# A third buffer for the output rows, a later place for the copies of v, and another cut of the last rows

## The chip, the cores and the metric

The kernel runs on one core of a Trainium2 chip. The metric is the device time of one execution in microseconds (us). A core has five engines that run their own instruction queues in order and meet at semaphores: TensorE (PE in the profile; its weight loads are shown apart as PEld), VectorE (DVE), ScalarE (ACT), GpSimd (POOL) and SyncE (SP, which here issues DMAs only).

## The reference, cut to what is computed

Sliding-window causal attention over 8 batches of 8 heads, 576 positions, head size 64, window 64, and then a layer x → (h·cos h)·w_out with h = x·w_in over the 4608 rows of 512 that come out of it.

```python
scores = scale * np.matmul(q, k.transpose(0, 1, 3, 2))
mask = (rel >= 0) & (rel < window)          # rel = row position - column position
scores = np.where(mask, scores, -1000000000.0)
attn = np.exp(scores - max); attn = attn / (sum + 1e-09)
x = np.matmul(attn, v)                      # 8 batches -> (4608, 512), heads side by side
h = x @ w_in                                # 512 -> 2048
out = (h * np.cos(h)) @ w_out               # 2048 -> 512, float32
```

## The kernel before

**Stages.** The 4608 rows are worked in nine stages of 512 rows (`mt`, 0 to 8). A stage has a first half, in which `h_ps` = w_in × xT is made for 16 blocks of 128 features (four matmuls of 512 columns each, L425), ScalarE takes the sine (L553; the cosine as a sine with an offset) and VectorE multiplies (L556, `gT`), and a second half, in which four blocks of 128 output rows are made, 16 matmuls of 512 columns each (L567). Each block is copied out of PSUM into half of a tile `out_sb` of 128 × 2 × 512 (L571): the even blocks by VectorE, the odd ones by ScalarE. Two blocks share one tile; in all stages but the last the tile is stored by one DMA of 512 KB that SP issues (`store`, L443), which is planned half a step to one step into the next stage. The pool has two buffers for these tiles (tag "out"). At the very start the same two buffers hold the plain float32 rows of q and k of the first two heads (`load_plain`, L160).

**Attention.** It runs a stage ahead: in stage t the attention of batch t + 1 is made while the matmuls above run. A batch has 8 heads in 4 pairs and 9 blocks of 64 rows; a unit is one pair and one block, a group three or four units, ten groups a batch. For a group TensorE makes the scores (L284), VectorE adds the mask and takes the maximum (L304), ScalarE takes exponentials and sums (L315), VectorE the reciprocals (L322), GpSimd multiplies (`g_norm`, L329, "normalisation", tile `w`), and SP issues a DMA transpose of `w` into `wT` (L341). At the end of a stage TensorE multiplies `wT` with v for the next stage's 512 rows (`values`, L356, 4 pairs of 16 matmuls), and the results are copied to `xT` (`put_x`, L361).

**q, k, v.** GpSimd issues the DMA loads, which cast to bfloat16: q and k in chunks of 96 rows two stages ahead of use (L174; 12 a stage), v in five chunks one stage ahead (L180). k is transposed by DMA on SP (`turn_k`, L244, six a batch), q on TensorE. A block of rows needs v of its own and of the preceding 64 positions, so a tile of v has 8 slots of 128 rows that overlap by 64: DMA fills the even slots, and `spread_v` (L184) builds the odd ones from them with two copies, one for each half of the partitions (64 × 1536 and 64 × 2048 elements). For batches 3 to 7 GpSimd makes these copies, one pair in each of stages 2 to 6.

**What sets the order.** Each engine runs its instructions in the order of the program. For the first stage that order is written out by hand (`FIRST`, L47). After it a list of steps with times (`at`, L449) is drained in order of time by `pump` (L452) between the matmuls of a stage; a stage is T = 32 units of planned time and t0 is its start. In stage t the groups' scores are planned from t0 + 14.6 on, 0.36 units for each unit of attention, the maxima 0.2, the exponentials 1, the reciprocals 3, the normalisations 3.2 and the transposes 3.8 later. The loads of q and k lie at t0 + 5.6 to 14.4, and the two copies of v at t0 + 14.45 and 14.55 (L492), ahead of the first normalisation.

**Which groups a stage's end needs.** In stages 3 to 6 the values of the next stage need the first four groups of the new batch; the other six belong to rows of the stage after. In stage 2 they need the first six (`CUTS`, L29).

**The last rows.** The last 128 rows of the last stage are split by columns (`last_rows`, L432): 16 matmuls for the first 448 columns, then 16 for the last 64. ScalarE copies and stores the first part, VectorE copies and SP stores the second.

Of the kernel before, what the change touches and what calls it, by code (L numbers as in the profile page):

```python
# [14 lines left out]
F32 = mybir.dt.float32  # L15
BF16 = mybir.dt.bfloat16
# [7 lines left out]
NU = 9  # L24
NC, NP = 6, 96
GF = 4
LAST = 448
PACE = 0.36
CUTS = (  # L29
# [7 lines left out]
RC = 9  # L37
PAIRS = 4
# [2 lines left out]
LAGS = (0.2, 1, 3, 3.2, 3.8)  # L41
SKEW = 3
DIRECT = (0, 7, 8)

# [28 lines left out]
def kernel(  # L73
# [10 lines left out]
    B, H, S, D = q.shape  # L84
    assert (B, H, S, D) == (8, 8, 576, 64)
    scale = 1.0 / math.sqrt(D)
    d_model = H * D
# [7 lines left out]
    const = ctx.enter_context(tc.tile_pool(name="const", bufs=1))  # L95
    ld = ctx.enter_context(tc.tile_pool(name="ld", bufs=2))
    att = ctx.enter_context(tc.tile_pool(name="att", bufs=3))
    moe = ctx.enter_context(tc.tile_pool(name="moe", bufs=2))
    ps = ctx.enter_context(tc.tile_pool(name="ps", bufs=1, space=PSUM))
    ps_t = ctx.enter_context(tc.tile_pool(name="ps_t", bufs=3, space=PSUM))  # L100

    qtiles = [const.tile([128, S], BF16, name=f"qT{i}") for i in range(2 * PAIRS)]
    qblocks = [const.tile([128, NU, 2, 64], BF16, name=f"qB{i}") for i in range(2 * PAIRS)]
    vtiles = [const.tile([128, NU - 1, d_model], BF16, name=f"v{i}") for i in range(2)]
    w_in_sb = const.tile([128, PAIRS, d_ff], BF16, name="w_in")
# [9 lines left out]
    st = {}  # L115
# [9 lines left out]
    def bank(which, name):  # L125
        return ps.tile([128, 512], F32, tag=which, name=name)

    def copy(engine, out, in_):
        {"a": nc.scalar.copy, "p": nc.gpsimd.tensor_copy}.get(engine, nc.vector.tensor_copy)(out, in_)  # L129
# [28 lines left out]
                            in_=src.rearrange("(a h) (p c) d -> (h p) a (c d)", h=2, c=RC))  # L158

    def load_plain(name):  # L160
        rows = moe.tile([128, 2, d_model], F32, tag="out", name="rows", bufs=2).rearrange("p a f -> p (a f)")[:, 0:RC * D]
        st["rows", name] = rows
        nc.sync.dma_start(out=rows, in_={"q": q, "k": k}[name][0, 0:2].rearrange("h (p c) d -> (h p) (c d)", c=RC))

# [94 lines left out]
    for b, cuts in enumerate(CUTS, 2):  # L259
        for cut in cuts:  # L260
            for p0 in range(0, PAIRS, 2):
                for of, lo, hi in cut:
                    groups += [[(b, p, j) for p in range(p, p + of) for j in range(lo, hi)] for p in range(p0, p0 + 2, of)]
    direct = set(range(n_first)) | {n_first + i for i in DIRECT}

# [144 lines left out]

    def put_out(m, engine=None):
        if ("osb", m // 2) not in st:
            st["osb", m // 2] = moe.tile([128, 2, d_model], F32, tag="out", name="out_sb", bufs=2)
        copy(engine, st["osb", m // 2][:, m % 2], st.pop(("out", m)))

    def exp_table():
        nc.scalar.activation(small, small, AF.Exp, scale=0.0)
# [4 lines left out]
    def first(mt, ff, ks, start, stop):  # L422
        if start:
            st["h", ff] = bank(H_BANKS[mt == 1][ff], "h_ps")
        nc.tensor.matmul(out=st["h", ff], lhsT=w_in_sb[:, ks, ff * 128:ff * 128 + 128],  # L425
                         rhs=st["xT", mt][:, ks], start=start, stop=stop)

    def skewed(mt, ks, n):
        for ff in range(SKEW):
            first(mt, ff, ks, n == 0, n == PAIRS - 1)  # L430

    def last_rows(gT, o_sb):  # L432
        ms = MT // 128 - 1
        for which, lo, hi in (("O0", 0, LAST), ("S", LAST, d_model)):
            o_ps = bank(which, "out_ps")[:, lo:hi]
            for ff in range(n_ff):
                nc.tensor.matmul(out=o_ps, lhsT=gT[ff // 2][:, ff % 2, ms * 128:ms * 128 + 128],  # L437
                                 rhs=w_out_sb[:, ff, lo:hi], start=ff == 0, stop=ff == n_ff - 1)
            to = moe.tile([128, MT], F32, tag="sin", name="last_sb", bufs=4)[:, lo:hi] if lo else o_sb[:, 1, lo:hi]
            copy("d" if lo else "a", to, o_ps)  # L440
            (nc.sync if lo else nc.scalar).dma_start(out=out[n_mt * MT - 128:n_mt * MT, lo:hi], in_=to)

    def store(o_sb, mt, ms0, e, n):  # L443
        r0 = mt * MT + (ms0 + e) * 128
        nc.sync.dma_start(out=out[r0:r0 + n * 128].rearrange("(a p) f -> p a f", p=128), in_=o_sb[:, e:e + n])
# [3 lines left out]
    def at(time, fn, *args):  # L449
        plan.append((time, len(plan), fn, args))  # L450

    def pump(time):  # L452
        plan.sort(key=lambda x: x[:2])
        while plan and plan[0][0] <= time:
            _, _, fn, args = plan.pop(0)
            fn(*args)
# [20 lines left out]
    for b in range(2, B):  # L477
        t0 = T * (b - 1)
        for p in range(PAIRS):
            t_q = t0 + (2 if b == 2 else 1) + (3.3 if b == 2 else 3.5) * p  # L480
            for lag, fn, *args in ((0, tr_q), (0.02, put_block, 0), (0.5, put_block, 1)):
                at(t_q + lag, fn, b, p, *args)
        if b > 2:
            for c in range(NC):
                for i, name in enumerate(("q", "k")):
                    at(t0 - T + 5.6 + 1.6 * c + 0.8 * i, load_chunk, name, b, c)
        for c in range(NC):
            at(t0 + (2 + 1.2 * c if b == 2 else c - 5.5), turn_k, b, c)
        for c in range(5):
            at(t0 + 0.5 + c, load_v, b, c)  # L490
        for half_ in range(2):
            at(t0 + (14.45 + 0.1 * half_ if b > 2 else 10), spread_v, b, half_, "p" if b > 2 else "s")  # L492
    for mt in range(2, n_mt):
        for p in range(PAIRS):
            time = T * mt - (8.01 if mt == n_mt - 1 else 1.01)
# [11 lines left out]
    def spread_first(lo, hi):  # L507
        return lambda i, engine: spread_v(0, i, engine, lo, hi)

    steps = {"Lq0": lambda p: load_heads("q", 0, p, 1) if p else load_plain("q"),  # L510
             "Lk0": lambda p: load_heads("k", 0, p, 1) if p else load_plain("k"),
             "cq": lambda engine: cast_plain("q", engine), "ck": lambda engine: cast_plain("k", engine),
             "Lq1": lambda p: load_heads("q", 1, p, 1), "Lk1": lambda p: load_heads("k", 1, p, 1),
# [23 lines left out]
    for mt in range(1, n_mt):  # L537
        base = mt * T
        gT = []
        for ks in range(PAIRS):  # L540
            pump(max([base - 1] + [time for time, _, fn, args in plan if fn is put_x and args[:2] == (mt, ks)]))
            skewed(mt, ks, ks)
        for ff in range(n_ff):
            for ks in range(PAIRS):
                if ff >= SKEW:
                    first(mt, ff, ks, ks == 0, ks == PAIRS - 1)
            h_ps = st.pop(("h", ff))
            sin = moe.tile([128, MT], F32, tag="sin", name="sin", bufs=4)
            if ff % 2 == 0:
                gt = moe.tile([128, 2, MT], BF16, tag="gT", name="gT", bufs=n_ff // 2 + 2)  # L550
                gT.append(gt)
            e = ff % 2
            nc.scalar.activation(sin, h_ps, AF.Sin, bias=math.pi / 2.0)  # L553
            if ff == n_ff - 1 and mt < B - 1:
                exp_table()
            nc.vector.tensor_tensor(out=gt[:, e], in0=h_ps, in1=sin, op=ALU.mult)  # L556
            pump(base + ff)
        for ms0 in range(0, MT // 128, 2):
            o_sb = moe.tile([128, 2, d_model], F32, tag="out", name="out_sb", bufs=2)
            o_ps = [bank(which, "out_ps") for which in (("O1",) if mt == n_mt - 1 and ms0 else ("O1", "O0"))]  # L560
            for e in range(2):
                ms = ms0 + e
                if mt == n_mt - 1 and ms == MT // 128 - 1:
                    last_rows(gT, o_sb)
                    break
                for ff in range(n_ff):
                    nc.tensor.matmul(out=o_ps[e], lhsT=gT[ff // 2][:, ff % 2, ms * 128:ms * 128 + 128],  # L567
                                     rhs=w_out_sb[:, ff], start=ff == 0, stop=ff == n_ff - 1)
                    if ff % 4 == 3:
                        if ff == n_ff - 1:  # L570
                            copy("a" if e else "d", o_sb[:, e], o_ps[e])  # L571
                            if mt == n_mt - 1:
                                store(o_sb, mt, ms0, e, 1)
                        pump(base + Q + 4 * ms0 + (e * n_ff + ff) // 4)
            if mt < n_mt - 1:
                at(base + T + 0.5 + ms0 / 2, store, o_sb, mt, ms0, 0, 2)
# [30 lines left out]
```

## Time and profile before

| | |
|---|---|
| time, three runs | 312.56, 314.43, 317.30 us; median 314.43 |
| profiled execution | 314.01 us, of which the span from first to last instruction 312.2 |
| busy time | TensorE 299.8, ScalarE 236.2, VectorE 229.4, GpSimd 192.3 us |
| DMA queues | GpSimd's 18.06 MB (84.4% of 16 engines' span), SP's 22.36 MB (36.9%) |
| L567 and L425, 1008 matmuls of 512 columns | 117.3 and 116.0 us busy |
| L329 normalisations on GpSimd | 75, mean 963 ns |
| L129 copies of v on GpSimd | 10, mean 1684 ns |
| L341 and L244, DMA transposes on SP | 68 of w and 36 of k, 3.9 and 7.5 us from issue to landing (median) |
| L445 stores of 512 KB on SP | 16, 7.8 us from issue to landing (median) |

The stages' bounds in the trace are 57.92 (stage 1), 90.50, 122.70, 154.74, 187.84, 220.04, 252.04 (stage 7) and 281.07 us (stage 8). A line of a timeline has start, duration, engine, source line, operation, output and inputs, and in brackets how long the engine sat idle before it and what ended that. L129 is the copy helper, so the tile tells which copy it is. An x2 means that two instructions are merged in one line. A line of the chain has start, duration and what ran. A line of the waits has the waiting instruction, what it waited for, the total, how often, and the longest.

### The profile page before, as it was taken

The page shows a single profiled execution, that of the slowest core. Times are in us where ns is not written, and L with a number is a line of the kernel's source. Part 1 is how long each engine was busy: PE and PEld are TensorE (multiplying, and loading weights), DVE is VectorE, ACT ScalarE, POOL GpSimd, SP SyncE. Part 2 cuts the span into 40 slices and gives each one's busy share as a digit, 9 for nine tenths or more (in the row PEclk, how much of TensorE's full clock was granted, in tenths as well). Part 3 has the DMA queues.
Part 4 walks back from the last instruction along what each step waited for, and adds up shares of the span by engine and source line. Part 5 has one row for each costly group of instructions (what it writes and reads, how often), then busy time and mean ns, then how long its engine had stood idle before and what let it go on. Part 6 is the DMA issues. An engine that isn't in the chain of part 4 may idle for free.

```text
span 312.2 us, 7988 instructions
## 1 busy us (share of the span) xinstructions
PE 299.8 (96%) x2659; PEld 161.5 (52%) x2659; DVE 229.4 (73%) x877; ACT 236.2 (76%) x785; POOL 192.3 (62%) x227
## 2 busy tenths in 40 slices
PE   3889999999999999999999899999999999999995
PEld 3668844545554555555555455454545554454443
DVE  5998988599769966897679667977698768235701
ACT  4998799777996799779977798689969986116600
POOL 8988666984679696958795978886842630000000
PEclk9979999999999999999999999999999999999999
DMA  8999999999979994999599979999894342011011
GB/s 158 178 217 170 200 177 140 122 143 194 219 108 142 159 191 78 133 128 231 88 116 129 228 109 100 135 228 123 99 127 151 68 117 91 0 69 68 0 69 67
DMA packets 155162, 41.17 MB, mean 132 GB/s; under 512 B 143408, under 2 KB 150384, under 8 KB 155120
## 3 DMA queue, kind: packets, MB, share of 16 engines
q0 software_dynamic: 100192, 18.06, 84.4%
q1 hardware_dynamic: 54784, 22.36, 36.9%
q8 instruction: 21, 0.34, 0.5%
q14 instruction: 21, 0.17, 0.2%
q10 hardware_dynamic: 144, 0.23, 0.2%
HBM read 36.70 MB, written 9.44 MB: 148 GB/s over the span
## 4 chain that ended last, share of the span: by engine, by line
PE 87%; DMA 4%; POOL 4%; DVE 1%; ACT 1%; issue 1%; DVEq 0%; POOLq 0%; ACTq 0%
PE h_ps L425 34%; PE out_ps L567 32%; PE h_ps L389 5%; PE s_ps L284 4%; PE out_ps L408 4%; PE o_ps L356 3%; DMA out_dram<-out_sb 3%; PE tq_ps L211 2%; POOL w L329 2%; DMA q<-in_q_dram 2%; POOL v L180 1%; PE out_ps L437 1%; PE s_ps L290 1%; PE tw_ps L338 1%; PE o_ps L375 1%
## 5 line engine op out<-in xcount | busy, mean ns | idle before, releaser
L567 PE MATMUL out_ps<-w_out,gT 128*128 128x512 bf16 x496 | 117.3, 379 | 0.0
L425 PE MATMUL h_ps<-xT,w_in 128*128 128x512 bf16 x512 | 116.0, 379 | 0.2
L315 ACT ACTIVATE e<-s,negm 128x128 f32<-128x128 f32 x256 | 98.7, 387 | 3.9 <-DVE negm L304 3.9
L553 ACT ACTIVATE sin<-h_ps 128x512 f32<-128x512 f32 x128 | 73.8, 598 | 32.1 <-PE h_ps L425 29.7
L556 DVE TENSOR_TENSOR gT<-h_ps,sin 128x512 bf16<-128x512 f32 x128 | 81.6, 685 | 21.8 <-ACT sin L553 21.0
L329 POOL TENSOR_TENSOR w<-e,rden 128x512 bf16<-128x512 f32 (+1 forms) x75 | 71.4, 963 | 32.9 <-DVE rden L322 26.3
L425 PEld LDWEIGHTS <-w_in 128*128 128x128 bf16 x512 | 48.5, 98 | 53.8 <-issue 0.4
L567 PEld LDWEIGHTS <-gT 128*128 128x128 bf16 x496 | 45.9, 98 | 44.2
L304 DVE CUSTOM_DVE_ANT_0 s<-s_ps,mask 128x128 f32<-128x128 f32 x256 | 58.2, 285 | 1.2 <-PE s_ps L290 1.0
L315 ACT ACTIVATION_READ_ACCUMULATOR e<-s,negm 128x1 f32 x256 | 47.8, 187 | 0.0
L174 POOL DMA_DIRECT2D q<-in_q_dram x36 | 28.5, 792 | 11.1 <-DMA q<-in_q_dram 5.3
L180 POOL DMA_DIRECT2D v<-in_v_dram x40 | 34.0, 866 | 0.6 <-DMA v<-in_v_dram 0.3
L174 POOL DMA_DIRECT2D k<-in_k_dram x36 | 28.3, 787 | 8.3 <-DMA k<-in_k_dram 4.4
L129 ACT COPY out_sb<-out_ps 128x512 f32<-128x512 f32 (+1 forms) x18 | 10.2, 567 | 25.0 <-PE out_ps L567 18.4
L322 DVE RECIPROCAL rden<-den 128x4 f32<-128x4 f32 (+1 forms) x79 | 13.6, 172 | 19.4 <-ACT e L315 18.9
L129 DVE COPY out_sb<-out_ps 128x512 f32<-128x512 f32 x18 | 12.4, 690 | 19.7 <-PE out_ps L567 12.0
L284 PEld LDWEIGHTS <-qB 128*128 128x128 bf16 x216 | 16.9, 98 | 15.8 <-DVE negm L304 2.4
L284 PE MATMUL s_ps<-kT,qB 128*128 128x128 bf16 x216 | 21.9, 219 | 1.0 <-DVE negm L304 0.9
L129 DVE COPY qB<-tq_ps 64x576 bf16<-64x576 bf16 x48 | 21.6, 450 | 0.3
L304 DVE DVE_READ_ACCUMULATOR2_ANT negm<- 128x1 f32 x256 | 21.3, 83 | 0.0
L129 DVE CAST xT<-o_ps 128x512 bf16<-128x512 f32 x24 | 15.5, 678 | 6.7 <-PE o_ps L356 6.7
L129 POOL COPY v<-v 64x1536 bf16<-64x1536 bf16 (+1 forms) x10 | 16.8, 1684 | 4.9 <-DMA v<-in_v_dram 4.6
(64 smaller groups left out, 253.4 us busy)
## 6 DMA issues: line engine op xcount, KB each, us to landing
out_dram<-out_sb SPq DMA_DIRECT2D x16, 512.0 KB, 7.8
v<-in_v_dram POOLq DMA_DIRECT2D x32, 128.0 KB, 5.7
q<-in_q_dram POOLq DMA_DIRECT2D x36, 96.0 KB, 9.1
k<-in_k_dram POOLq DMA_DIRECT2D x36, 96.0 KB, 8.9
w_in<-in_moe_w_in_dram POOLq DMA_DIRECT2D x4, 512.0 KB, 8.5
w_out<-in_moe_w_out_dram POOLq DMA_DIRECT2D x4, 512.0 KB, 10.8
wT<-w SPq DMA_TRANSPOSE x68, 3.9
q<-in_q_dram POOLq DMA_DIRECT2D x7, 144.0 KB, 5.6
```

The source lines that it names most:

```text
L129: {"a": nc.scalar.copy, "p": nc.gpsimd.tensor_copy}.get(engine, nc.vector.tensor_copy)(out, in_)
L174: nc.gpsimd.dma_start(out=st[name, b][:, c].rearrange("p (h d) -> p h d", h=H), in_=src.rearrange("h p d -> p h d"))
L180: nc.gpsimd.dma_start(out=vt.rearrange("p (h d) -> p h d", h=H), in_=v[b, :, c * 128:c * 128 + n, :].rearrange("h p d -> p h d"))
L284: nc.tensor.matmul(out=s_ps[:, u].rearrange("p (a t) -> p a t", a=2), lhsT=qblocks[(b % 2) * PAIRS + p][:, j].rearrange("d h t -> d (h t)" ...
L304: nc.vector.tensor_tensor_reduce(out=s[:, u], in0=s_ps[:, u], in1=mask[:, 2 - j % 2 if j else 0], scale=-scale if b else -1.0, scalar=BIG, ...
L315: nc.scalar.activation(e[:, u], s[:, u], AF.Exp, bias=negm[:, u:u + 1], scale=1.0 if n < n_first else -1.0, accum_out=den[:, u:u + 1])
L329: (nc.gpsimd if engine == "p" else nc.vector).tensor_tensor(out=w[:, 0:u], in0=e[:, 0:u], op=ALU.mult, in1=rden[:, 0:u].unsqueeze(2).to_br ...
L389: nc.tensor.matmul(out=h_ps[:, half * e:half * e + half], lhsT=w_in_sb[:, ks, ff * 128:ff * 128 + 128], rhs=st["xT", 0][:, ks, half * g:ha ...
L425: nc.tensor.matmul(out=st["h", ff], lhsT=w_in_sb[:, ks, ff * 128:ff * 128 + 128], rhs=st["xT", mt][:, ks], start=start, stop=stop)
L553: nc.scalar.activation(sin, h_ps, AF.Sin, bias=math.pi / 2.0)
L556: nc.vector.tensor_tensor(out=gt[:, e], in0=h_ps, in1=sin, op=ALU.mult)
L567: nc.tensor.matmul(out=o_ps[e], lhsT=gT[ff // 2][:, ff % 2, ms * 128:ms * 128 + 128], rhs=w_out_sb[:, ff], start=ff == 0, stop=ff == n_ff - 1)
```

## The change

Three edits, cut from the diff:

```diff
-LAST = 448
+LAST = 384
...
+OUTS = 3
...
-    qtiles = [const.tile([128, S], BF16, name=f"qT{i}") for i in range(2 * PAIRS)]
+    first_q = moe.tile([128, 2, d_model], F32, tag="out", name="qT", bufs=OUTS).rearrange("p a f -> p (a f)").bitcast(BF16)
+    qtiles = [first_q[:, S * i:S * i + S] for i in range(PAIRS - 1)]
+    qtiles += [const.tile([128, S], BF16, name=f"qT{i}") for i in range(PAIRS - 1, 2 * PAIRS)]
...
-        rows = moe.tile([128, 2, d_model], F32, tag="out", name="rows", bufs=2).rearrange("p a f -> p (a f)")[:, 0:RC * D]
+        rows = moe.tile([128, 2, d_model], F32, tag="out", name="rows", bufs=OUTS).rearrange("p a f -> p (a f)")[:, 0:RC * D]
...
-            st["osb", m // 2] = moe.tile([128, 2, d_model], F32, tag="out", name="out_sb", bufs=2)
+            st["osb", m // 2] = moe.tile([128, 2, d_model], F32, tag="out", name="out_sb", bufs=OUTS)
...
-            at(t0 + (14.45 + 0.1 * half_ if b > 2 else 10), spread_v, b, half_, "p" if b > 2 else "s")
+            at(t0 + (22.2 + 0.1 * half_ if b > 2 else 10), spread_v, b, half_, "p" if b > 2 else "s")
...
-            o_sb = moe.tile([128, 2, d_model], F32, tag="out", name="out_sb", bufs=2)
+            o_sb = moe.tile([128, 2, d_model], F32, tag="out", name="out_sb", bufs=OUTS)
```

The tag "out" gets three buffers in place of two. Each is 4096 bytes a partition; to make room, the transposed q of the first three pairs of batch 0 (3 × 1152 bytes), which had tiles of their own for the whole kernel, lies in the first of the three buffers until the first output rows take it over. The pair of copies of v of batches 3 to 7 is planned at t0 + 22.2 and 22.3, between the fourth normalisation (t0 + 22.12, in stage 2 t0 + 21.4) and the fifth. The last 128 rows are split into 384 and 128 columns.

## The prediction

> **What bounds the kernel now.** I read the table of engines first (TensorE busy for 299.8 of the 312.2 us span), then the stretches of stages 2 to 6, the steady ones in which the change works (stage = the loop variable mt; the cuts are where the chain shows the first h_ps group of each).
>
> ```profile
> core 0: us, PE busy (x) PEld busy (x) DVE busy (x) ACT busy (x) POOL busy (x), PEclk, DMA share, GB/s
> 90.50:122.70 32.20, 32.18 (x254) 16.76 (x254) 25.50 (x112) 28.08 (x97) 26.01 (x30) 1.00 1.49 140
> 122.70:154.74 32.04, 32.01 (x253) 16.52 (x254) 25.28 (x112) 26.72 (x92) 26.12 (x29) 1.00 1.54 142
> 154.74:187.84 33.10, 32.14 (x252) 16.57 (x252) 25.50 (x112) 27.38 (x95) 26.23 (x29) 1.00 1.54 142
> 187.84:220.04 32.20, 32.14 (x252) 16.56 (x253) 25.51 (x112) 27.39 (x95) 26.02 (x29) 1.00 1.63 144
> 220.04:252.04 32.00, 31.97 (x252) 16.66 (x253) 25.83 (x112) 27.99 (x98) 17.31 (x18) 1.00 0.81 111
> ```
>
> The reader is to see that a stage lasts as long as its matmuls, about 32.0 us at a granted clock of 1.00, except stage 4, which lasts 33.10. No other engine reaches 29 us. So there is little to win: what lies above 32.0 is 0.20, 0.04, 1.10, 0.20 and 0. The chain of waits says what the 1.10 is, and the list of waits how often its cause occurs:
>
> ```profile
> 167.16 1.74 PE h_ps L425 x8
> 169.09 7.99 DMA out_dram<-out_sb
> 177.33 0.45 issue
> 178.82 0.40 PE s_ps L284 x4
> ```
> ```profile
> DVE out_sb L129 <- DMA out_dram<-out_sb: 7.2, 4, 2.6
> PE s_ps L284 <- DVE negm L304: 0.9, 1, 0.9
> ```
>
> The stores of the stage before stand in SP's queue behind ten transposes of w and six of k, and in stage 4 are issued at 169.09, 14 us into the stage. They land 8 to 9 us later, and the first output copy of the stage, on VectorE, needs that buffer. The timelines of VectorE and TensorE there, and GpSimd's:
>
> ```profile
> 177.17 0.69 DVE L129 COPY out_sb<-out_ps 128x512 f32<-128x512 f32 x1 [2.56 <-DMA out_dram<-out_sb]
> 178.82 0.40 PE L284 MATMUL s_ps<-kT,qB 128*128 128x128 bf16 x4 [0.94 <-DVE negm L304]
> ```
> ```profile
> 173.54 3.43 POOL L129 COPY v<-v 64x1536 bf16<-64x1536 bf16 x2
> 177.06 3.03 POOL L329 TENSOR_TENSOR w<-e,rden 128x512 bf16<-128x512 f32 x3
> ```
>
> VectorE stands still for 2.56 us; behind the copy in its queue lie the reciprocal and the maxima of the next groups, so a bank of scores is freed late and TensorE stops. The same wait lasts 1.43, 1.55 and 1.65 us in stages 2, 3 and 5 and hardly reaches TensorE (in stage 5 one group of four score matmuls takes 0.40 us of the chain in place of 0.22). So some 1.5 us of such a wait is covered, and all beyond it costs TensorE one for one: 2.56 - 1.5 = 1.06.
>
> **Part 1, the third buffer.** Buffers now go round in three: the first pair of rows of a stage takes the buffer of the second pair of two stages earlier, whose store landed a stage ago; the second pair takes that of the first pair of the stage before. The closest case is stage 4: that store is issued at 169.09, lands by 178.1, and the copy that needs it is the third of the stage, which came after 180.94. So all four waits (7.2 us of VectorE) go. Worth on TensorE: 1.0 us in stage 4 (33.10 less the mean 32.15 of stages 2, 3 and 5 is 0.95; by the cover 1.06) and 0.2 in stage 5 (0.40 - 0.22): 1.2. The ends are 0.95 (stage 4 alone) and 1.54 (each of the four falls to stage 6's 32.00). What is late next is nothing on VectorE; TensorE's own matmuls are.
>
> The price is that three tiles of q of batch 0 share the first buffer. The first output copy, at 46.09, must then wait for their last score matmuls; those (group 8, eight matmuls) ended at 43.83 and stand ahead of the matmuls that the copy waits for anyway: 0. The plain rows of q and k take buffers 2 and 3 at the start, both free: 0. Whether a write of one of the three q tiles waits for reads of another the trace can't show. Upper end: the second VectorE write (9.66 to 10.40) would wait for the scores that end at 10.35, 0.7 us, on a start whose chain runs through loads and GpSimd; lower end 0, since nothing gets earlier. I take 0: kT and xT are written by slices of one tile in the same way, and no wait of a writer for a reader of another slice is listed.
>
> **Part 2, the two copies of v.** Nothing is added: ten instructions stay ten, and no DMA moves. In stages 2 to 6 the pair (3.43 us in stage 4, 3.41 in stage 6) moves past four normalisations on GpSimd; no load lies between. The first normalisation of stage 4 then needs only its reciprocal (173.54) and starts at about 173.8, not 177.06. With ScalarE's pace of 1.54 us a group (four exponentials at 0.387) the fourth ends at 179.6, the copies at 183.1, and the fifth starts at 183.2, not 181.2. SP hardly feels it: its transposes take 1.2 to 2.4 us each, and in the old order it fell behind GpSimd with every one (the fifth normalisation of stage 4 was done at 182.2, its transpose issued at 184.48). The new order has the first four early and the fifth at 184.3. The tenth normalisation waits for its reciprocal (188.55) in both orders, so the loads behind it don't move. What waits for the copies are the value matmuls at the stage's end. Ends of the copies, from each stage's own reciprocals, against first use (a stage's TensorE moved earlier by its saving): 117.6 against 121.3, 150.7 against 153.6, 183.1 against 185.6, 216.1 against 218.7, 248.2 against 250.9. The least margin is 2.5 us. Cover is thinner in stage 2: there the values also need groups 5 and 6, and the sixth transpose, issued at 119.68, is what the value matmuls wait for now (a piece of 0.02 us of issue at 122.12 in the chain). The sixth normalisation would end at 119.4 and not at 117.06, and SP take it at 119.5 to 119.8: between -0.2 and +0.3 us, I take 0.1. Sum of part 2: +0.1, ends -0.2 and +0.5.
>
> One sentence from the Trainium skill speaks against moving GpSimd's work about: SBUF — State Buffer, section "Who interferes with whom", says that VectorE and GpSimd share a port pair, and that a VectorE instruction with two SBUF inputs, or in a two-port mode, shuts GpSimd out for its whole length. By that rule with such neighbours the pair could take twice 3.43 us; here the rule and the rows agree on no loss, since the maxima (s_ps and mask) and the output copies (out_ps) that lie beside the new place read at most one operand from SBUF.
>
> **Part 3, the last rows.** The chain gives 3.51 us for the 32 matmuls. At the 512-column rate (0.86 us for four) 16 of 448 columns are 3.02, which leaves 0.49 for those of 64. New: 16 of 384 are 2.59 and, at the rate of the 128-column scores (0.22 for four), 16 of 128 are 0.88: 3.47, so -0.04. VectorE's last copy took 0.225 us for 64 columns and 0.690 for 512, so 128 take 0.29: +0.07. ScalarE's part ends 0.45 earlier, but the other store is last (issued 309.02 against 308.87). Landing: 2.1 us for 32 KB, 2.0 for 256 KB, so 64 KB cost nothing. Sum +0.03, ends -0.2 and +0.2 (the landing's spread on both sides).
>
> DMA: Bandwidth & Descriptors of the Trainium skill, section "Specifications", puts the line rate at runs of 512 B and more; the last store goes from 256 to 512 B a row, which by that rule would be a gain. The two landings of 2.1 and 2.0 us leave no more than 0.1 for it.
>
> **Sum.** The profiled execution took 314.01 us: span 312.2 and 1.81 around it. 314.01 - 1.2 + 0.1 + 0.03 = 312.9; I forecast 312.8, since the three runs shown (312.56, 314.43, 317.30) spread over 4.7 us and every microsecond by which a store lands later than here would have cost one in up to four stages, and that source goes. The median of the runs, 314.43, is 0.4 above the profiled execution.
>
> **Rivals.**
> - The gain is given back. Groups 5 and 6 behind the copies hold the end of stage 2 (up to 0.5), the shared q buffer holds the start (up to 0.7): 312.9 + (0.5 - 0.1) + 0.7 = 314.0, no change. For it: stage 2 has no slack at its end now. Against: SP was 2.6 us behind GpSimd there.
> - The copies of v become the wait (the other side). If the pair takes 6.9 us and not 3.43, the values of stages 3 to 6 start 0.5, 0.9, 0.8 and 0.7 us late and stage 2's sixth group 3.4: 6.3, so 319.1, slower. It decides once the pair ends 2.5 us later than I have it, through length or a late start. Against: the pair lasted 3.43 beside maxima and 3.41 beside gating products; a late start of GpSimd by up to 2 us falls into the gaps of 0.5 us between its normalisations.
> - The third buffer changes nothing, because the wait is for something else. Against: the lines name the store, and 169.09 + 8 is 177.1. Then 314.1.
> - More than forecast: in the runs shown late stores cost more than in the profiled one, and the ends of the sums fall well: 314.01 - 1.54 - 0.2 - 0.2 = 312.1; from the fastest run, 312.56 less 1.2 is 311.4.
>
> **How the numbers follow.** Forecast (312.2 to 313.5): 0.55. Given back (313.5 to 315): 0.15; nothing done: 0.05. More than forecast (311.3 to 312.2): 0.13. Copies of v late (315 and up): 0.10; something unseen: 0.02. Range 311.3 to 315.0, which holds 0.88 before I allow for the runs' own spread; it is nearer 0.8 with it. The forecast's own range is 312.2 to 313.5. Two per cent, 6.3 us, is about what a measurement of this kernel can tell from no change; faster by that needs more than all that stages 2 to 6 have above 32.0 each (only the unseen: 0.02), and slower needs the copies later still than in the rival (half of its chance: 0.05), so within 2% has 0.93.
>
> **What would show it.** Part 1 is right if no output copy waits for a store and stage 4 lasts 32.1 us; wrong if VectorE still waits there, or SP's order has shifted the stores. Part 2 is right if four normalisations precede each pair, the pair still takes 3.4 us, and the value matmuls of stages 2 to 6 show no new wait; the sixth transpose of stage 2 should start at 119.5 to 119.8 less any shift. Part 3 is right if 32 matmuls take about 3.47 us and the last store ends the run. The prediction is wrong above all if the end of a stage waits for v or for wT.

## The result and the profile after

The changed kernel takes 312.72 us (median of 22 runs, 311.29 to 314.00), the kernel before 314.49 us (22 runs, 312.56 to 319.90). The ratio is 0.9933 with a 95% interval of 0.9913 to 0.9952, a gain of 0.5 to 0.9%, so within the 2% bound. Ratios and their intervals are estimated from the fast runs alone (runs over 1.5% above the fastest of their kernel count as slow), so they are not the quotients of the medians. The profiled execution after took 313.61 us with a span of 311.8, against 314.01 and 312.2 before.

The stretches of stages 2 to 6 of after, with the columns as before (length first, then busy time and instructions of each engine):

```profile
core 0: us, PE busy (x) PEld busy (x) DVE busy (x) ACT busy (x) POOL busy (x), PEclk, DMA share, GB/s
92.11:124.11 32.00, 31.76 (x249) 16.63 (x253) 25.71 (x112) 27.97 (x98) 26.05 (x30) 1.00 1.46 142
124.11:156.10 31.99, 31.75 (x249) 16.64 (x252) 25.74 (x112) 27.36 (x95) 25.76 (x29) 1.00 1.64 144
156.10:188.09 31.99, 31.76 (x248) 16.65 (x252) 25.74 (x112) 27.37 (x95) 26.13 (x30) 1.00 1.59 144
188.09:220.09 32.00, 31.76 (x249) 16.66 (x253) 25.83 (x112) 27.37 (x95) 26.12 (x30) 1.00 1.49 146
220.09:252.08 31.99, 31.75 (x249) 16.63 (x252) 25.88 (x112) 27.36 (x95) 16.89 (x18) 1.00 0.82 109
```

All five stages last 32.0 us; the 33.10 of stage 4 is gone. The third buffer is seen at work in VectorE's timeline of stage 4, and the new place of the copies in GpSimd's:

```profile
175.89 0.68 DVE L132 COPY out_sb<-out_ps 128x512 f32<-128x512 f32 x1
```
```profile
175.16 1.04 POOL L332 TENSOR_TENSOR w<-e,rden 128x512 bf16<-128x512 f32 x1
176.74 1.04 POOL L332 TENSOR_TENSOR w<-e,rden 128x512 bf16<-128x512 f32 x1 [0.54 <-DVE rden L325]
178.24 1.04 POOL L332 TENSOR_TENSOR w<-e,rden 128x512 bf16<-128x512 f32 x1 [0.46 <-DVE rden L325]
179.78 1.04 POOL L332 TENSOR_TENSOR w<-e,rden 128x512 bf16<-128x512 f32 x1 [0.50 <-DVE rden L325]
180.76 3.41 POOL L132 COPY v<-v 64x1536 bf16<-64x1536 bf16 x2
184.25 4.18 POOL L332 TENSOR_TENSOR w<-e,rden 128x384 bf16<-128x384 f32 x5
```

The output copy has no bracket, so VectorE didn't idle before it, though the two stores of the stage before were issued at 169.94 and 170.58 and took 8.4 and 9.4 us to land, as late as ever and after that copy had begun. Four normalisations precede the pair of copies, the second to the fourth waiting only for their reciprocals, and five run in one piece behind it.

But the span is only 0.4 us shorter, because this execution began worse. Its chain at the end of the first stage:

```profile
52.22 5.68 DMA wT<-w
57.95 0.66 PE o_ps L359 x30
```

TensorE waited 1.46 us for a transposed tile of w. Stage 1 began at 59.86, and at 58.19 in the execution before. The experiments show how much that varies.

The tail. First the DMA issues of before (last column: us from issue to landing), then the timeline and the DMA issues of after:

```profile
out_dram<-out_sb ACTq DMA_DIRECT2D x1, 224.0 KB, 2.1
out_dram<-last_sb SPq DMA_DIRECT2D x1, 32.0 KB, 2.1
```

```profile
308.42 0.37 ACTq L444 DMA_DIRECT2D out_dram<-out_sb  x1
309.13 0.33 SPq L444 DMA_DIRECT2D out_dram<-last_sb  x1
```
```profile
out_dram<-out_sb ACTq DMA_DIRECT2D x1, 192.0 KB, 1.9
out_dram<-last_sb SPq DMA_DIRECT2D x1, 64.0 KB, 1.6
```

Before, both stores landed in 2.1 us and were issued 0.15 us apart (308.87 and 309.02); now they are 0.71 apart and take 1.9 and 1.6. From the start of the last 32 matmuls, as the chain gives it, to the end of the span it is 311.8 - 305.28 = 6.52 us, against 312.2 - 305.24 = 6.96.

### The profile page after: what moved, and what is told of

It is laid out like the page before. It is cut to its first block, busy times and chain, and to the rows that moved or that the text cites. A ratio compares the mean times of both kernels' runs of the same rounds, so it can differ in the third digit from the quotient of the medians.

```text
span 311.8 us, 7954 instructions
## 1 busy us (share of the span) xinstructions
PE 296.8 (95%) x2627; PEld 161.6 (52%) x2659; DVE 230.6 (74%) x877; ACT 236.1 (76%) x785; POOL 191.7 (61%) x227
## 4 chain that ended last, share of the span: by engine, by line
PE 83%; DMA 8%; ACT 3%; POOL 3%; DVE 1%; issue 1%; SPq 1%; POOLq 0%; DVEq 0%; ACTq 0%
PE h_ps L428 34%; PE out_ps L570 34%; DMA w_in<-in_moe_w_in_dram 4%; PE s_ps L287 4%; PE h_ps L392 3%; PE o_ps L359 3%; ACT e L318 2%; PE tq_ps L214 2%; DMA wT<-w 2%; DMA k<-in_k_dram 2%; POOL v L183 1%; PE out_ps L440 1%; PE out_ps L411 1%; DVE s L307 1%; SPq L344 1%
## 5 line engine op out<-in xcount | busy, mean ns | idle before, releaser
L570 PE MATMUL out_ps<-w_out,gT 128*128 128x512 bf16 x482 | 116.1, 379 | 0.8 <-issue 0.2
L559 DVE TENSOR_TENSOR gT<-h_ps,sin 128x512 bf16<-128x512 f32 x128 | 81.6, 685 | 21.4 <-ACT sin L556 20.6
L307 DVE CUSTOM_DVE_ANT_0 s<-s_ps,mask 128x128 f32<-128x128 f32 x256 | 58.5, 286 | 1.2 <-PE s_ps L293 1.0
```

The lines of the kernel that those rows point to most:

```text
L307: nc.vector.tensor_tensor_reduce(out=s[:, u], in0=s_ps[:, u], in1=mask[:, 2 - j % 2 if j else 0], scale=-scale if b else -1.0, scalar=BIG, ...
```

## The experiments

All stages are measured alike in what follows: from the start of a stage's first h_ps matmul in TensorE's timeline to the next one's. "Tail" is the end of the span less the start of the last 32 matmuls in the chain; the span is printed to 0.1 us, so a tail is good to about 0.05. For each kernel one profiled execution is measured; medians are of its timed runs, with the ratio to runs of the kernel before that were timed beside them (the experiments' had medians of 313.98 to 314.35).

| kernel | stage 1 begins | stages 1, 2, 3, 4, 5, 6 (us) | tail | median or one run | ratio (95%) |
|---|---|---|---|---|---|
| before | 58.19 | 32.26, 32.17, 32.12, 33.10, 32.20, 32.00 | 6.96 | 314.49 | |
| after | 59.86 | 32.25, 32.00, 31.99, 31.99, 32.00, 31.99 | 6.52 | 312.72 | 0.9933 (0.9913 to 0.9952) |
| buffer alone | 58.93 | 32.25, 32.00, 31.99, 31.99, 32.00, 31.99 | 7.05 | 312.74 | 0.9959 (0.9923 to 0.9995) |
| copies alone | 57.99 | 32.26, 33.85, 32.01, 32.48, 32.47, 32.00 | 6.94 | 315.82 | 1.0084 (1.0052 to 1.0115) |
| cut alone | 57.48 | 32.26, 32.00, 31.99, 32.91, 31.99, 31.99 | 6.58 | 313.18 | 0.9978 (0.9944 to 1.0013) |
| early stores | 59.31 | 34.03, 32.01, 32.00, 31.99, 31.99, 32.00 | 6.98 | 315.30 | 1.0046 (1.0015 to 1.0077) |
| early stores from stage 2 | 58.47 | 32.25, 32.00, 32.00, 31.99, 31.99, 32.00 | 7.01 | 313.56 | 0.9973 (0.9942 to 1.0004) |
| copies made twice | 59.40 | 32.25, 35.49, 34.05, 33.17, 33.69, 32.01 | 6.54 | 321.70 (one) | |
| copies behind the sixth | 59.20 | 32.26, 31.99, 32.00, 31.99, 31.99, 32.00 | 6.57 | 312.05 | 0.9945 (0.9922 to 0.9968) |
| copies behind the eighth | 58.80 | 32.25, 34.34, 36.46, 34.78, 33.69, 31.99 | 6.59 | 323.87 (one) | |
| one group direct | 57.55 | 32.25, 32.00, 31.99, 32.00, 31.99, 31.99 | 6.63 | 312.09 | 0.9944 (0.9916 to 0.9972) |
| direct, behind the sixth | 58.57 | 32.26, 31.99, 32.00, 31.99, 31.99, 32.00 | 6.60 | 312.22 | 0.9932 (0.9905 to 0.9960) |
| last store in 256-byte runs | 58.62 | 32.26, 32.00, 32.00, 31.99, 31.99, 31.99 | 6.65 | 312.49 (one) | |
| 448 and 64, stores apart | 57.34 | 32.26, 31.99, 32.00, 31.99, 32.00, 31.99 | 6.93 | 311.49 (one) | |

**The third buffer alone.** From the changed kernel:

```diff
-LAST = 384
+LAST = 448
-            at(t0 + (22.2 + 0.1 * half_ if b > 2 else 10), spread_v, ...
+            at(t0 + (14.45 + 0.1 * half_ if b > 2 else 10), spread_v, ...
```

> The third buffer alone: the copies of v stay ahead of the first normalisation, the last rows stay at 448 and 64 columns. Theory (the late store is the whole loss of stages 2 to 6): no output copy waits for a store, stages 2 to 6 last 32.0 us each, 159.9 to 160.1 together against 161.5 before, and the time falls by 1.5 us, about 313.0. Rival (the place of the copies of v is what counts): the waits for the store go, but normalisations behind the copies still hold TensorE, some stage stays at 32.5 or more, and the time falls by less than 0.8 us. Second rival (the shared q buffer costs up to 0.7 us at the start): stages at 32.0, but the time falls by 0.8 only.

No output copy waits for a store, and stages 2 to 6 take 159.97 us together, as after, against 161.59. The theory holds for the stages. Whether the shared q buffer costs at the start the time doesn't tell: the median fell by 1.33, but the interval (0.9923 to 0.9995, a gain of 0.2 to 2.4 us) takes in both 0.8 and 1.5. The trace of after tells it for the place that was feared, in VectorE's and TensorE's lines:

```profile
9.64 0.75 DVE L231 TENSOR_SCALAR qT<-tq_ps 128x576 bf16<-128x576 bf16 x1
10.40 0.41 PE L293 MATMUL s_ps<-kT,qT 64*64 64x128 bf16 x8
```

The second VectorE write of a q tile begins without idle time ahead of it, while scores that stand before it in the program and read another of the three tiles begin only at 10.40. So it waits for no reader of another tile. It begins at 9.59 to 9.70 in the nine profiles with the shared buffer and at 9.55 to 9.79 in the five without.

**The later copies alone.** From the kernel before:

```diff
-            at(t0 + (14.45 + 0.1 * half_ if b > 2 else 10), spread_v, ...
+            at(t0 + (22.2 + 0.1 * half_ if b > 2 else 10), spread_v, ...
```

> The later copies of v alone: two buffers, last rows at 448 and 64. Theory: VectorE still waits for the store in stages 2 to 5, 1.4 to 2.6 us each, since SP ends its queue no earlier; one stage or two stay longer than 32.1 us and the time is that of before, 314.5 within 0.4. Rival (the copies are what counts): stages at 32.0 and the time falls by 1.2 us or more, to 313.2.

Both times were wrong: it is slower, by 0.5 to 1.2%. Stage 2 alone grew by 1.7 us. Its end in TensorE's timeline, and GpSimd's lines ahead of it:

```profile
121.01 0.89 PE L356 MATMUL o_ps<-wT,v 128*64 128x64 bf16 x44
123.61 0.55 PE L356 MATMUL o_ps<-wT,v 128*64 128x64 bf16 x20 [1.72 <-DMA wT<-w]
```
```profile
111.97 2.61 POOL L329 TENSOR_TENSOR w<-e,rden 128x384 bf16<-128x384 f32 x3 [2.15 <-DVE rden L322]
114.52 3.40 POOL L129 COPY v<-v 64x1536 bf16<-64x1536 bf16 x2
118.01 5.98 POOL L329 TENSOR_TENSOR w<-e,rden 128x384 bf16<-128x384 f32 x6
```

Behind an output copy before which VectorE idled 1.57 us the reciprocals came late, so normalisations 2 to 4 began 2.15 us after GpSimd was free, the pair of copies behind them ended 27.7 us into the stage (26.7 in after), and the sixth normalisation, which ended at 120.13 by the chain, 29.9 us into it. The last transposed tile that this stage's values need then came too late. With the copies ahead of the first normalisation the same wait of VectorE runs beside the copies and costs nothing there (the cut alone, below, has the same 1.57 us in stage 2, which lasts 32.00). So the later place is free only together with the third buffer. In stages 4 and 5 the wait for the store was 1.93 us each and the stages 0.48 and 0.47 longer than 32.0.

**The cut alone.** `LAST = 384` in the kernel before.

> The cut of the last rows at 384 alone. Theory from the two traces: TensorE's 32 matmuls take 3.5 us as before, the last store is issued 0.05 to 0.1 us later and lands in 1.6 to 1.7 us and not 2.1, so the time falls by 0.4 us, to 314.1. Rival (the prediction's own step: landing doesn't depend on size): landing 2.0 to 2.1 us and the time as before within 0.1.

The last store landed in 1.6 us and the tail is 6.58 us, 0.38 shorter than before: the theory. The median fell by 0.9 with an interval that holds 0.4 and zero. In this execution VectorE idled 1.57, 0.34, 2.36 and 0.68 us before the first output copy of stages 2, 3, 4 and 5, and only stage 4 was longer than 32.0, by 0.91.

**The early store, with two buffers.** From the kernel before:

```diff
-                at(base + T + 0.5 + ms0 / 2, store, o_sb, mt, ms0, 0, 2)
+                at(base + (25.2 if ms0 == 0 else T + 0.5), store, o_sb, mt, ms0, 0, 2)
```

> Two buffers and all else as before, but the store of the first pair of rows of a stage stands in SP's queue behind the fifth or sixth transpose of its own stage and not behind all ten and the six of k. Theory (a late store, not the number of buffers, is the cause): the store is issued some 20 us earlier, no output copy waits for one, stages 2 to 6 last 32.0 to 32.1 us each and the time falls by 1.5 us, to 313.0, like the third buffer alone. Rival (it is the missing buffer, or SP's load): copies still wait over 1 us, or SP held by the store delays the transposes and a stage's end, and the time stays at 314.5 or rises.

Stages 2 to 6 are at 32.0 without a third buffer, so the lateness of the store is the cause; yet the kernel is slower. Stage 1 lost 1.8 us, as SP's and TensorE's lines show:

```profile
88.49 0.53 SPq L445 DMA_DIRECT2D out_dram<-out_sb  x1
89.11 1.40 SPq L341 DMA_TRANSPOSE wT<-w  x1
```
```profile
92.91 0.51 PE L356 MATMUL o_ps<-wT,v 128*64 128x64 bf16 x20 [1.68 <-DMA wT<-w]
```

The sixth transpose of stage 1, which its values need, stands behind the store in SP's queue. It is issued 29.8 us into the stage, 0.7 later than in the kernel before (at 87.28, 29.1 us into it), and lands 3.75 us after its issue and not 2.69. With stage 1 left as it was:

```diff
+                at(base + (25.2 if mt > 1 and ms0 == 0 else T + 0.5), store, o_sb, mt, ms0, 0, 2)
```

> The kernel before with two buffers and only the store of the first pair of rows of stages 2 to 7 moved ahead in SP's queue; stage 1, where the early store cost 1.8 us by holding the sixth transpose, is left as it was. Theory (the late store is the cause, and the order in SP's queue cures it as well as a buffer does): stage 1 at 32.26, stages 2 to 6 at 32.0 and the time 1.3 us below before, 312.7. Rival (in stage 2 too the store ahead of the sixth transpose holds the end of the stage): stage 2 at 33 or more, time 313.8 or more.

Stage 1 is back at 32.25 and stages 2 to 6 at 32.0, so the cure by order works for the stages as the buffer does. The time is 0.8 us below before with an interval that reaches just past zero; the expected 1.3 lies inside it.

**Where the copies become the wait.** In the changed kernel each copy of v made twice; then planned at t0 + 24.8; then at t0 + 27.5:

```diff
             copy(engine, to, of)
+            if b > 2:
+                copy(engine, to, of)
```

> The changed kernel with each of the ten copies of v made twice, so that the pair takes 6.8 us. Theory (the pair ends 2.8 us ahead of the values of stages 3 to 6 in the changed kernel's trace, and stage 2's sixth normalisation has no margin): stages 3 to 6 grow by 6.8 - 3.4 - 2.8 = 0.6 us each and stage 2 by 3 to 3.4, together 5.5 to 6, time near 318.5. Rival (the copies hold nothing, since odd slots are needed late in the value matmuls): stages 3 to 6 stay at 32.0 and only stage 2 grows.

It cost more than either said, 8.4 us in stages 2 to 5. TensorE's lines of the ends of stages 2 and 3:

```profile
126.48 0.73 PE L361 MATMUL o_ps<-wT,v 128*64 128x64 bf16 x20 [3.18 <-DMA wT<-w]
...
160.16 1.01 PE L361 MATMUL o_ps<-wT,v 128*64 128x64 bf16 x52 [0.43 <-POOL v L132]
```

Stage 2 lost 3.5 us, nearly all to the sixth transpose, as forecast (3 to 3.4). Stage 3 waited 0.43 at its end for v itself. Most of the rest of its 2.1 was lost in its first 3 us, and not in a wait for data: from 126.66 to 130.07 the clock that TensorE was granted was 0.50 of full speed, and matmuls of 512 columns began 0.43 us apart, not 0.22. That stretch of 3.41 us costs some 1.7 us (an estimate, half its length), which leaves 6.7 of the 8.4 for the copies. Stage 4 waited 0.40 for v and 0.48 for a transposed tile of w, stage 5 1.32 for a transposed tile. Stage 6 lost nothing, though its pair ended at 259.61 (252.73 and 6.88) and its values had begun at 258.83: they don't read the slots that are copied.

> The changed kernel with the copies of v behind the sixth normalisation (planned at t0 + 24.8), so that the pair ends 2.6 us later. Theory (2.8 us of margin at the end of stages 3 to 6): stages 2 to 6 stay within 0.3 us of 32.0, time 312.7 as after, stage 2 with more margin for its sixth transpose. Rival (the margin is smaller than the trace shows, since the semaphore and the copies of several slots come in between): stages 3 to 6 grow by 0.5 us or more each and the time by 2 us.

The theory. In stage 3 the pair ended at 154.09 and the values began at 154.22, and no stage grew:

```profile
150.68 3.41 POOL L132 COPY v<-v 64x1536 bf16<-64x1536 bf16 x2
```
```profile
154.22 1.20 PE L359 MATMUL o_ps<-wT,v 128*64 128x64 bf16 x64
```

> The changed kernel with the copies of v behind the eighth normalisation (planned at t0 + 27.5), so that the pair ends 5.5 to 6 us later than after, near 33.8 us into a stage whose values begin at 30.8. Theory: each of stages 2 to 6 grows by 2.7 to 3.2 us, time near 327. Rival (TensorE has other work to put in between, or the values read the odd slots last): growth under 1.5 us a stage.

The waits came in stages 2 to 4 (2.15, 2.63 and 2.60 us for v, the stages growing by 2.3, 4.5 and 2.8); the expectation was wrong for 5 and 6. TensorE's lines of the ends of stages 3 and 5, and GpSimd's of stage 5:

```profile
160.81 1.01 PE L359 MATMUL o_ps<-wT,v 128*64 128x64 bf16 x52 [2.63 <-POOL v L132]
...
229.09 1.20 PE L359 MATMUL o_ps<-wT,v 128*64 128x64 bf16 x64
```
```profile
228.99 3.41 POOL L132 COPY v<-v 64x1536 bf16<-64x1536 bf16 x2
```

In stage 5 the values ran while the pair was being copied. The code says why: from batch 6 they read blocks 0 and 1, both from slot max(j - 1, 0) = 0, which DMA fills; from batch 7 block 0 alone. What stage 5 lost (1.7) was lost in its first microseconds, as a stretch of its busy times shows (columns as in the stretches above; PEclk, the granted clock of TensorE, is the third number from the end):

```profile
197.00:200.40 3.40, 3.18 (x9) 1.21 (x8) 0.84 (x3) 1.28 (x1) 3.06 (x4) 0.50 0.44 73
```

At half the clock 3.4 us of matmuls cost 1.7 more. Another such stretch, from 125.32 to 128.74, accounts for nearly all that stage 3 lost beyond its wait for v. Why the clock was halved isn't shown: in this profile it was after the waits that ended at 124.32 and 195.63, and stayed at 1.00 after the longest, which ended at 160.81.

**One group of the first stage by TensorE.** In the changed kernel:

```diff
-DIRECT = (0, 7, 8)
+DIRECT = (0, 5, 7, 8)
-... Gn.16.d Gw.8 Gc.14 Gc.13 Lk2.0 Gp.8.d o.3.2 ...
+... Gn.16.d Gw.8 Gw.13 Gc.14 Lk2.0 Gp.8.d Gp.13.d o.3.2 ...
```

> The changed kernel, and in the first stage one group more (the four blocks of the third pair of batch 1) is transposed by TensorE and copied by VectorE, not by a DMA on SP. In the traces of after, of the buffer alone, of the copies alone and of the early stores TensorE waits 1.4 to 1.7 us for that group's transposed tile at the end of the first stage, in the two others it doesn't. Theory (that wait is a matter of the DMA queues of the run and is the larger part of what differs between runs at the start): it is gone, four transposes cost 0.2 us, the third stage starts at 90.3 to 90.8 us instead of 92.1, and the median falls by 0.8 us, to 311.9. Rival (something else is late next, such as VectorE or the next group's transpose): the start is no earlier and the time 312.7 or a little more.

The wait is absent here, and stage 2 begins at 89.80 and not 92.11. But the expectation counted the copies alone among those that have it by mistake (that wait is the one of stage 2). Of the twelve profiles without this edit seven show the wait, of 0.26 to 1.56 us, and five don't (before, copies alone, cut alone, copies behind the eighth, stores apart). The ratio, 0.9944, is not to be told from that of after, so that the edit makes the runs faster isn't shown.

**Both edits together.** The copies behind the sixth normalisation and the direct group.

> The changed kernel with the copies of v behind the sixth normalisation and the one group of the first stage transposed by TensorE. Theory: the two edits touch different stages; stages 2 to 6 stay at 32.0, no wait for a transposed tile at the end of the first stage, median 311.8 to 312.1. Rival (copies that end 0.1 us ahead of the values are late in some runs): median above 312.3.

312.22 us, between the theory's upper end and the rival. All stages are at 32.0 and no transposed tile was waited for, but the ratio, 0.9932 (0.9905 to 0.9960), is that of after. No version of these beats the changed kernel by a measurable amount.

**The last store.** Runs of 256 bytes with 128 columns, then 64 columns with the stores apart, both in the changed kernel:

```diff
-            to = moe.tile([128, MT], F32, tag="sin", name="last_sb", bufs=4)[:, lo:hi] if lo else o_sb[:, 1, lo:hi]
+            to = moe.tile([128, MT], F32, tag="sin", name="last_sb", bufs=4)[:, 0:256].rearrange("p (a f) -> p a f", a=2)[:, :, 0:64] if lo else o_sb[:, 1, lo:hi]
```

> The changed kernel with the last 128 columns held as two pieces of 64, so that the last store moves runs of 256 bytes on the SBUF side, in the same 64 KB, and is issued 0.7 us behind ScalarE's store as in after. So far the last store landed in 2.1 us in all four profiles with 64 columns (issued 0.15 us behind ScalarE's) and in 1.6 us in all six with 128 (0.7 us behind). Theory (it stood behind ScalarE's store in the DMA engines): 1.6 to 1.7 us again. Rival (runs of 512 bytes are what made it faster): 2.0 us or more.

```profile
out_dram<-last_sb SPq DMA_DIRECT2D x1, 64.0 KB, 1.7
```

```diff
-LAST = 384
+LAST = 448
-            copy("d" if lo else "a", to, o_ps)
+            for _ in range(3 if lo else 1):
+                copy("d" if lo else "a", to, o_ps)
```

> The changed kernel with the last rows at 448 and 64 columns again and VectorE's last copy made three times, so that the last store is issued 0.6 us behind ScalarE's and not 0.15. Theory (distance): it lands in 1.6 to 1.7 us, so that the run ends no later than with one copy. Rival (row size): 2.1 us, and the run ends 0.45 us later than with one copy.

```profile
out_dram<-out_sb ACTq DMA_DIRECT2D x1, 224.0 KB, 2.0
out_dram<-last_sb SPq DMA_DIRECT2D x1, 32.0 KB, 1.5
```

Both landings are as the distance theory has them: 128 columns in 256-byte runs land in 1.7 us, 64 columns issued 0.67 us behind ScalarE's store in 1.5. Two needless copies, 0.5 us of VectorE, cost the tail nothing (6.93 us against 6.94 to 7.05 with one copy). But the distance gained nothing either. Here as in the kernel before the last store lands 0.15 to 0.2 us behind ScalarE's (before: 309.02 + 2.1 against 308.87 + 2.1; here: 307.07 + 1.5 against 306.40 + 2.0). With 448 columns the run ends at the same time after ScalarE's store at both distances.

## Why the prediction was right, point by point

**The level.** 312.8 was forecast, 312.72 measured. The agreement is better than the working, and so in part luck. The forecast lies 1.2 below the profiled execution, which itself lay 0.5 below the median of the 22 runs, and that median fell by 1.77: a base 0.5 too low and a gain 0.6 too small cancelled.

**Part 1: mechanism right, term too small.** The store's lateness is the cause: removing it by a buffer or by SP's order brings all stages to 32.0. Forecast 1.2 (ends 0.95 and 1.54), measured 161.59 - 159.97 = 1.62. The mis-sized term is that of stages 2 and 3, for which I counted nothing and which gave 0.17 and 0.13; stage 4 gave 1.11 and stage 5 0.20. That stage 2's 0.17 was the store's isn't shown: in the kernel before, TensorE's only stop there is the one at the sixth transposed tile (at 122.14), and the cut alone, where VectorE idled as long before the output copy, has stage 2 at 32.00. The cover of 1.5 us, read off three waits, held in other executions: 1.23 us of wait (early stores from stage 2, in stage 2) cost nothing, 1.93 cost 0.48 and 0.47 (1.93 - 1.5 = 0.43), and 2.36 cost 0.91 (0.86).

**Part 1, shared q buffer: nothing where it was feared.** The write that was to wait up to 0.7 us didn't wait (9.64 in after, 9.66 before), and the first output copy, at 46.10, waited for its own matmuls. So 0 was the right price for both. The start as a whole can't say more: stage 1 began at 57.34 to 59.86 in the nine profiles with the buffer (mean 58.7, or 58.9 without the two that have the direct group) and at 57.48 to 59.31 in the five without (mean 58.3).

**Part 2: right in the sum, wrong where it stands alone.** Forecast +0.1, measured 0.0: the stages of after and of the buffer alone agree within 0.01 us. The pair takes 3.41 us in its new place and 6.86 when doubled, so no shut-out by VectorE shows; by the Trainium skill's rule on the port pair (SBUF — State Buffer, "Who interferes with whom") there should be none beside VectorE instructions with one operand from SBUF that use no two-port mode, and the trace agrees. What the prediction missed is that the two parts depend on each other. It named stage 2's sixth transpose as the thin place and priced it at 0.1 with the buffer. Without the buffer that place costs 1.7 us.

**Part 3: the failed step is "but the other store is last".** Forecast +0.03 (ends -0.2 and +0.2), measured -0.41: the mean tail is 6.58 us in five profiles with 384 columns (after, the cut alone, behind the sixth, the direct group, both together) and 6.99 in five with 448 (before, buffer, copies, the two with early stores). The matmuls took 3.51 us, as before (3.47 forecast). The prediction noted that ScalarE's part ends 0.45 us earlier and then set it aside, because the other store is issued last, and gave that store a fixed 2.1 us. But that landing isn't fixed: 0.15 us behind a store of 224 KB it takes 2.1 us, 0.7 us behind one of 192 KB 1.6. And the distance alone isn't the gain: putting the two stores apart without making ScalarE's earlier left the tail at 6.93. What the cut at 384 adds to the distance is that ScalarE's store is smaller and issued 0.5 us earlier (308.42 - 305.28 = 3.14 us after the last 32 matmuls begin, not 308.87 - 305.24 = 3.63). So the 0.45 us that were set aside are about the gain of 0.41. DMA: Bandwidth & Descriptors of the Trainium skill (section "Specifications") would give the gain to runs of 512 bytes; runs of 256 landed in 1.7 and 1.5 us, so the measurement decides against that here.

**The rivals.** "Given back" didn't happen in after (stage 2 at 32.00); alone, the copies cost 1.7 us in stage 2. "Copies become the wait" was priced at 6.3 us for a doubled pair and took 8.4, of which some 1.7 is the halved clock; the remaining 6.7 is near the price, with another split (stages 4 and 5 waited for transposed tiles too). The margin was read rightly for stages 2 to 4 (copies that end 0.13 us ahead of the values cost nothing), and wrongly for 5 and 6, whose values read no copied slot. "More than forecast" is true of the stages' and the tail's terms (1.62 + 0.41 = 2.03), less so of the time.

**What stays open** is the cause of the uneven start. In 14 profiles stage 1 begins anywhere from 57.34 to 59.86. Two things go with it. The seven profiles in which TensorE waits for a transposed tile of w at the end of the first stage begin stage 1 at 59.1 in the mean, the seven without at 58.0. Of the seven without it, three (before, copies behind the eighth, both together) have a stretch of 3.41 us from 18.7 to 19.5 on in which the granted clock was 0.50; they begin at 58.5 in the mean and the other four at 57.6. Among the 22 runs of the changed kernel the six with a mean clock of 0.995, which is what one such stretch makes of a whole run, have a median of 312.9 us, the 16 with 0.999 or 1.000 one of 312.3. Why the tile is late, and the clock halved, in some executions and not in others wasn't found.

## What to carry to other kernels

A wait that hardly touches the bounding engine may be just covered: here some 1.5 us of a late store were free and what lay beyond cost one for one, so remove it for what the runs can bring and not for what one profile charges. Before work is moved later in a queue, take the latest release that the queue already suffers and see whether it now lies ahead of the moved work instead of beside it. At the end of a kernel look at when the larger of the last stores is issued, not only at the last one: here making it smaller and 0.5 us earlier gained 0.4, and putting the two apart without that gained nothing. And look at the granted clock of a stretch before its length is put down to a wait.

## What the runs showed of the hardware that I had not expected

- A store of 32 KB issued 0.15 us behind one of 224 KB from another queue landed in 2.1 us in five profiles, 0.67 us behind it in 1.5, both times 0.15 to 0.2 us after the larger one. One of 64 KB, 0.7 us behind one of 192 KB, landed in 1.6 us in seven, and in 1.7 in runs of 256 bytes. Why is not shown.
- In four of the 14 profiles the granted clock fell to 0.50 for stretches of 3.41 us (one each in before, copies made twice and both together, three in copies behind the eighth), and where matmuls of 512 columns ran in them they began 0.43 us apart and not 0.22. Not every long wait of TensorE was followed by one.
- The start of the kernel varied by 2.5 us between executions, while every undisturbed middle stage repeated within 0.02 us.
